# First block: TensorE's third exchanged first, a weight unit split sooner, one tap on ScalarE; last round of the last block by halves of the tokens

## The chip, the core and the metric

The kernel runs on one core of one Trainium2 chip. The metric is the device time of one execution in microseconds (us). Five engines work side by side, each through its own queue in program order: TensorE (PE in the profile; its weight loads stand as PEld), VectorE (DVE), ScalarE (ACT), GpSimd (POOL) and SyncE (SP), which here only issues transfers. Semaphores hold an instruction back until what it needs is done.

## The reference

A depthwise causal convolution over 4096 tokens with 7 taps, whose weights are a softmax for each of 8 heads, feeds a feed-forward layer with a gated activation. All is float32.

```python
B, S, D = 8, 4096, 192            # x; H, K = 8, 7; d_ff = 2048
w = softmax(weight)               # [8, 7], one row for 24 channels
out[b, s, c] = sum_k w[c // 24, k] * x_pad[b, s + k, c]
h = out.reshape(32768, 192) @ w_in          # [32768, 2048]
g = h * np.clip(h + 3, 0, 6) / 6
return g @ w_out                            # [32768, 192]
```

The weights of both products come as float64 and are brought to float32 on the chip from their two 32-bit words.

## The kernel before

The 32768 tokens go in 32 blocks of 1024, two halves of 512 tokens. x lies with channels on partitions: 64 partitions for the lower half of the tokens, 64 for the upper, and three "thirds" of 64 channels side by side in the free dimension (`y[:, 0..2]`). `swap(third)` (L273) exchanges the two partition halves through two DMAs on SyncE's queue (L276, L277), so that each half of the partitions holds the other half's tokens as well: OWN is what a partition half computed, OTHER is what it got.

**h of a block.** A product of h takes 64 rows of a weight unit against 512 tokens (`half_mm`, L302, matmul on L311); two such products, one on each half of the rows, run side by side. The result goes through ScalarE's relu (L317) and VectorE's gate (L321) into `g`. PSUM has eight banks, handed out by `take` and given back by `give` after the gate.

**The first block** is written out by hand, from L653 on. Its order is the program order of each engine:

- *Convolution.* The last third (`pe_third`) is convolved by TensorE: seven diagonal matrices, made by ScalarE (L670), times shifted x (L671); ScalarE copies the sum out of PSUM (L684). The other two thirds are convolved by VectorE, seven taps each in two halves of 256 tokens, so 14 steps a third (`per`): the first tap is a multiplication (L259), the others multiply and add (L263).
- *Weights.* 16 units, 8 of w_in and 8 of w_out. `split` is two VectorE operations (L174, L178), `clamp` three of ScalarE (L186, L189, L192), `join` two of VectorE (L195, L199), of which the second needs clamp's last result, and a product on GpSimd (L203), whose result the matmuls read. `load(n)` issues a unit's transfers on SyncE's queue.
- *Mixing.* The loop over `conv0` puts splits, clamps and joins between the taps: split(0) and clamp(0) before step 5, join(0) before step 11; before step 14 the copy of TensorE's third, the exchange of the first third and then of TensorE's, load(4), split(1) and clamp(1); before step 20 split(2), join(1), clamp(2); after the taps the exchange of the middle third, split(3), split(4), join(2), clamp(3).
- *First products.* Four parts (weight units 0 and 1, for OWN and for OTHER) take all eight banks; thirds come in `order = (0, pe_third, 1)`, the middle third last. After it come relu and gate for part after part, with a split, a join and a clamp beside some of them (`slots`, `between`), and twelve more parts, each with three pairs of products.

`out_direct` then makes the first block's output; the other blocks compute h by hand-written plans (`h_phase`) and the output by a seven-product scheme with fewer matmuls (`out_strassen`).

**The last block's output** is `out_last`. A round is one bank: four column tiles of 32 rows, each the sum of 8 matmuls (`mm`, L437) over 512 tokens, started in turn so that four run side by side (`side_by_side`). VectorE adds and subtracts rounds into c tiles (`add`, L541), `store` transposes 32x32 blocks (L547) and issues one DMA for each 32 channels (`store_rows`, L455). The last round is

```python
b, bank = three(3, 4, 2)
add(u2[:], u2[:], bank[m])                       # m: rows 0 to 95
store(i, u2, 0, 1, queues=both)                  # SyncE and ScalarE queues in turn
add(u3[rows(2)], u3[rows(2)], bank[rows(NQ)], ALU.subtract)   # rows 96 to 127
store(i, u3, 1, 0, range(2, 3), queues=both[::-1])
give(b)
```

Before it VectorE adds the quarters of product 5 (`pieces`), and stores `p5`.

Of the kernel before, what the change touches and what calls it, by code (L numbers as in the profile page):

```python
# [16 lines left out]
def kernel(  # L17
# [21 lines left out]
    nc = tc.nc  # L39
# [115 lines left out]
    class Rounding:  # L155
# [10 lines left out]
        def load(self):  # L166
            self.st = self.load_words()
# [105 lines left out]
    def swap(part):  # L273

        to = slice(OTHER + part.start, OTHER + part.stop)
        nc.sync.dma_start(out=y[D2:P, to], in_=y[0:D2, part])  # L276
        nc.sync.dma_start(out=y[0:D2, to], in_=y[D2:P, part])  # L277
# [19 lines left out]
    def take():  # L297
        return free_banks.pop(0)
# [131 lines left out]
    def dff_half(k):  # L430
        return g[:, :, k // G, k % G]

    def mm(bank, j, x, w, q, ps_, first, last):

        cols = slice(q * QS, (q + 1) * QS)
        return [
            lambda p=p: nc.tensor.matmul(  # L437
                out=bank[j * QS : (j + 1) * QS], lhsT=w_out[:, p, w, cols], rhs=x[:, p],
                start=(first and p == ps_[0]), stop=(last and p == ps_[-1]),
                tile_position=(0, j * QS),  # L440
            )
            for p in ps_
        ]

    def side_by_side(*streams):
        for mms in zip(*streams):
            for m in mms:
                m()

    every = range(NP)  # L450

    def store_rows(i, k, q, xt, j, dma=nc.sync):

        t0 = i * TB + k * N
        dma.dma_start(  # L455
            out=out[t0 : t0 + N, q * QS : (q + 1) * QS].rearrange("(t r) d -> r t d", r=QS),
            in_=xt[j * QS : (j + 1) * QS].rearrange("r (t d) -> r t d", d=QS),
        )

    def out_direct(i, work):  # L460
# [41 lines left out]
        5: (None, T1), 6: (S2, T2), 7: (S3, T3),  # L502
    }

    def product(bank, j, n, q, ks=every):
        x, w = prod[n]
        return mm(bank, j, S1 if n == 5 else x, w, q, ks, True, True)

    def four(*parts):

# [5 lines left out]
    def three(n, n4, q4):  # L516
        return four(*[(n, q) for q in range(NQ)], (n4, q4))
# [11 lines left out]
    def rows(q):  # L529
        return slice(q * QS, (q + 1) * QS)  # L530
# [9 lines left out]
    def add(out, x, y, op=ALU.add):  # L540
        nc.vector.tensor_tensor(out=out, in0=x, in1=y, op=op)  # L541

    def store(i, c, k, half_, qs=range(NQ), queues=(nc.sync,)):

        xt = ot.tile([P, N], F32, name="xt")
        r = slice(qs[0] * QS, (qs[-1] + 1) * QS)
        nc.vector.transpose(out=xt[r], in_=c[r])  # L547
        for q in qs:
            store_rows(i, k, half_ * NQ + q, xt, q, queues[q % len(queues)])

    def sums_tiles():
        return (cs.tile([DH, N], F32, name=f"c{k}") for k in range(6))
# [3 lines left out]
    def out_last(i):  # L556

        both = nc.sync, nc.scalar
        p1, p2, p4, p5, u2, u3 = sums_tiles()
        b, bank = three(1, 2, 0)  # L560
        nc.scalar.copy(out=p1[:], in_=bank[m])
        piece(p2, 0, bank, NQ)
        give(b)
        g_sums(nc.vector, (2,), every, 4)
        b, bank = four((2, 1), (2, 2), (4, 0), (4, 1))
        for dst, q, j in ((p2, 1, 0), (p2, 2, 1), (p4, 0, 2), (p4, 1, 3)):
            piece(dst, q, bank, j)
        give(b)
        g_sums(nc.vector, (4,), every, 4)
        add(p2[:], p1[:], p2[:])  # L570
        store(i, p2, 0, 0)
        b7, bank7 = three(7, 5, 0)
        piece(p5, 0, bank7, NQ)
        b, bank = three(6, 5, 1)
        piece(p5, 1, bank, NQ)
        add(u2[:], p1[:], bank[m])
        give(b)
        add(u3[:], u2[:], bank7[m])
        give(b7)
        two = slice(0, 2 * QS)  # L580
        add(p4[two], u3[two], p4[two], ALU.subtract)
        store(i, p4, 1, 0, range(2))
        b, bank = by_quarters(5, 2)
        pieces(p5, 2, bank)
        give(b)
        add(u2[:], u2[:], p5[:])
        add(p5[:], u3[:], p5[:])
        store(i, p5, 1, 1)
        b, bank = three(3, 4, 2)
        add(u2[:], u2[:], bank[m])  # L590
        store(i, u2, 0, 1, queues=both)
        add(u3[rows(2)], u3[rows(2)], bank[rows(NQ)], ALU.subtract)
        store(i, u3, 1, 0, range(2, 3), queues=both[::-1])
        give(b)

    def out_strassen(i, conv):
# [56 lines left out]
    with tc.manual_schedule():  # L653
        nc.vector.tensor_reduce(out=sm[:], in_=e_sb[:], axis=AX.X, op=ALU.add)
        nc.vector.tensor_scalar_add(sm[:], sm[:], 1e-9)
        nc.vector.reciprocal(sm[:], sm[:])
        nc.vector.tensor_tensor(
            out=c_sb[:], in0=e_sb[:], in1=sm[:].to_broadcast([P, KC]), op=ALU.mult
        )

        thirds = [slice(s, s + 1) for s in range(K3)]
        pe_third = K3 - 1
        b = take()
        for _ in range(3):

            nc.tensor.matmul(
                out=psum[:, b], lhsT=zeros[:, 0:P], rhs=zeros[:], start=True, stop=True
            )
        for k in range(KC):
            nc.scalar.mul(diag[:, k], ident[:], c_sb[:, k : k + 1])  # L670
            nc.tensor.matmul(  # L671
                out=psum[:, b], lhsT=diag[:, k], rhs=x_tiles[0][:, pe_third, k : k + N],
                start=(k == 0), stop=(k == KC - 1),
            )
        conv0 = conv_units(0, thirds[:pe_third], 2)
        per = len(conv0) // pe_third
        for k, u in enumerate(conv0):
            if k == 5:
                split(0)
                clamp(0)  # L680
            elif k == per - 3:
                join(0, more=False)
            elif k == per:
                nc.scalar.copy(out=y[:, pe_third], in_=psum[:, b])  # L684
                give(b)
                swap(thirds[0])
                swap(thirds[pe_third])
                load(AHEAD)
                split(1)
                clamp(1)  # L690
            elif k == per + 6:
                split(2)
                join(1)
                clamp(2)
            u()
        swap(thirds[1])
        split(3)
        split(4)
        join(2)
        clamp(3)  # L700


        parts = [(c, group) for p in range(0, NP, 2) for group in (OWN, OTHER)
                 for c in (p, p + 1)]
        early = [(c, group, (take(), take())) for c, group in parts[:4]]
        order = (0, pe_third, 1)
        for c in range(2):
            for slot, group, bs in early:
                if slot == c:
                    for s in order[:2]:  # L710
                        h_mm(c, group, bs, s, order)
        for c, group, bs in early:
            h_mm(c, group, bs, order[2], order)

        slots = [0, 1, 2, 3, 5, 6, 8, 10, 12, 14]
        n = 3
        for slot, (c, group) in enumerate(parts):
            first = slot < len(early)
            if first:
                bs = early[slot][2]  # L720
            else:
                bs = take(), take()
                for s in range(K3):
                    h_mm(c, group, bs, s)
            more = slot in slots

            def between():
                if more:
                    join(n)
                    clamp(n + 1)  # L730

            if slot == 6:
                x_tiles[1] = load_x(1)
            h_out(c, group, bs, (lambda: None) if first else between)
            if more:
                split(n + 2)
                if first:
                    between()
                n += 1
        while n < len(units):  # L740
            join(n)
            clamp(n + 1)
            split(n + 2)
            n += 1
        w_sums()
        start_pools.close()
        ss = ctx.enter_context(tc.tile_pool(name="ss", bufs=1))
        p5s = ctx.enter_context(tc.tile_pool(name="p5s", bufs=3))
        cs = ctx.enter_context(tc.tile_pool(name="cs", bufs=1))
        ot = ctx.enter_context(tc.tile_pool(name="ot", bufs=4))  # L750

        def conv_and_swap(i):
            return conv_units(i, [slice(0, K3)]) + [lambda: swap(slice(0, K3)), y_sums]

        out_direct(0, conv_and_swap(1))
        x_tiles[2] = load_x(2)

        S1 = ss.tile([P, NP, N], F32, name="s1")[:]
        left = []
        for i in range(1, NB):  # L760
            h_phase(left)
            if i + 1 < NB:
                left = out_strassen(i, conv_units(i + 1, [slice(0, K3)]))
            else:
                out_last(i)
            if i + 2 < NB:
                x_tiles[i + 2] = load_x(i + 2)
# [33 lines left out]
```

## Time and profile before

| | us |
|---|---|
| median of 6 runs (lowest to highest) | 2410.85 (2410.79 to 2410.95) |
| the profiled execution's own time | 2410.83 |
| its span, first to last instruction | 2409.0 |
| TensorE busy (share of the span) | 2398.3 (100%) |
| VectorE busy | 2088.1 (87%) |
| ScalarE busy | 1076.9 (45%) |
| GpSimd busy | 673.0 (28%) |
| TensorE's first product of h starts | 14.35 |
| first block's first output matmul starts | 58.75 |
| last matmul of the last round ends | 2402.79 |

A timeline line reads: start, length, engine, line, operation, output<-inputs, shapes, count, and in brackets the idle time of the engine before it with what ended it. The chain of waits is followed back from the last instruction: at each step to what released it, else to the instruction before it on its engine. The granted clock is the share of TensorE's full clock that it was given. A float32 matmul stands as two MATMUL records.

### The profile page before, as it was taken

To read this page: it belongs to the slowest core of one execution; us is meant where nothing else is said; L and a number is where in the kernel's file an instruction comes from. 1 tells how busy PE (TensorE), PEld (TensorE's weight loads), DVE (VectorE), ACT (ScalarE), POOL (GpSimd) and SP (SyncE) were. 2 spreads that over 40 slices of the span, in tenths; PEclk is the share of its full clock that TensorE was granted. 3 is DMA by queue.
4 is the path that set the end of the run, shared out by engine and by line. 5 is a ranking of instruction groups with operands and counts; after the bars stand their busy time and mean duration, and the time that the engine had idled before them with its cause. 6 is when DMAs were issued, how large, how long until landed. Compare 5 with 4: busy or idle time off the path is not lost.

```text
span 2409.0 us, 40076 instructions
## 1 busy us (share of the span) xinstructions
PE 2398.3 (100%) x16468; PEld 1009.2 (42%) x16468; DVE 2088.1 (87%) x2534; ACT 1076.9 (45%) x1827; POOL 673.0 (28%) x280
## 2 busy tenths in 40 slices
PE   9999999999999999999999999999999999999998
PEld 4334444334444344443444434444334444344433
DVE  8788888988888888898888898888898888888896
ACT  7234553345543355433454334553335543355433
POOL 2523321233221333122332223322233312333122
PEclk9999999999999999999999999999999999999999
DMA  5211122101122011221112211122201122111210
GB/s 145 40 25 29 27 40 40 39 18 26 39 41 40 19 35 27 40 41 22 32 27 40 41 34 22 27 40 40 40 18 34 30 40 40 21 34 27 40 27 14
DMA packets 227336, 84.65 MB, mean 35 GB/s; under 512 B 205456, under 2 KB 210576, under 8 KB 227152
## 3 DMA queue, kind: packets, MB, share of 16 engines
q1 hardware_dynamic: 225848, 81.56, 17.1%
q8 instruction: 129, 2.11, 0.4%
q14 instruction: 55, 0.45, 0.1%
q10 hardware_dynamic: 1208, 0.27, 0.1%
q0 software_dynamic: 96, 0.26, 0.0%
HBM read 31.72 MB, written 25.17 MB: 24 GB/s over the span
## 4 chain that ended last, share of the span: by engine, by line
PE 99%; DVE 1%; DMA 0%; issue 0%; ACTq 0%; SPq 0%; DVEq 0%
PE psum L311 50%; PE psum L437 48%; DVE y L263 0%; DMA x<-in_x_dram 0%; DMA y<-y 0%; DVE c L541 0%; ACTq L92 0%; DVE scale L174 0%; DVE y L259 0%; DVE scale L195 0%; DVE sig L199 0%; DVE top L178 0%; DVE xt L547 0%; SPq L276 0%; DVEq L259 0%
## 5 line engine op out<-in xcount | busy, mean ns | idle before, releaser
L437 PE MATMUL psum<-g,w_out 128*32 128x512 f32 x9312 | 1163.6, 592 | 0.0
L311 PE MATMUL psum<-y,w_in 64*128 64x512 f32 x3664 | 884.1, 591 | 3.0 <-DVE y L263 1.8
L497 POOL TENSOR_TENSOR s<-g 128x1024 f32<-128x1024 f32 x124 | 293.6, 2368 | 1644.7 <-DVE g L321 1644.7
L317 ACT ACTIVATE r<-psum,half 128x512 f32<-128x512 f32 x1024 | 641.2, 688 | 241.3 <-PE psum L311 234.1
L437 PEld LDWEIGHTS psum<-g,w_out 128*32 128x32 f32 x9312 | 337.4, 110 | 811.7 <-issue 770.2
L321 DVE SCALAR_TENSOR_TENSOR g<-r,psum 128x512 f32<-128x512 f32 x1024 | 641.2, 680 | 5.0 <-ACT r L317 1.1
L437 PE MATMUL psum<-s,w_out 128*32 128x512 f32 x1488 | 638.5, 592 | 0.0
L311 PEld LDWEIGHTS psum<-y,w_in 64*128 64x128 f32 x3664 | 430.2, 187 | 378.6 <-issue 298.8
L311 PE MATMUL psum<-y,w_in_t 64*128 64x512 f32 x1984 | 523.9, 592 | 0.0
L403 DVE TENSOR_TENSOR psum<-psum,p 128x512 f32<-128x512 f32 x496 | 324.5, 694 | 196.5 <-PE psum L311 187.5
L263 DVE SCALAR_TENSOR_TENSOR y<-x,c_sb,y 128x1536 f32<-128x1536 f32 (+1 forms) x210 | 416.7, 1992 | 6.6
L533 ACT COPY c<-psum 32x512 f32<-32x512 f32 x188 | 108.7, 578 | 600.7 <-PE psum L437 600.0
L497 POOL TENSOR_TENSOR g<-g 128x1024 f32<-128x1024 f32 x124 | 338.3, 2728 | 9.7
L311 PEld LDWEIGHTS psum<-y,w_in_t 64*128 64x128 f32 x1984 | 247.4, 186 | 194.0 <-issue 124.8
L541 DVE TENSOR_TENSOR c<-c,psum 32x512 f32<-32x512 f32 (+1 forms) x187 | 128.1, 685 | 81.6 <-ACT c L533 75.7
L396 ACT COPY psum<-psum 128x512 f32<-128x512 f32 x248 | 138.9, 571 | 72.5 <-PE psum L311 57.5
L437 PEld LDWEIGHTS psum<-s,w_out 128*32 128x32 f32 x1488 | 162.4, 110 | 1.2 <-issue 1.2
L399 ACT COPY p<-psum 128x512 f32<-128x512 f32 x248 | 133.2, 591 | 40.9 <-PE psum L311 40.1
L497 DVE TENSOR_TENSOR g<-s,g 128x2048 f32<-128x2048 f32 x62 | 139.3, 2286 | 3.9 <-POOL g L497 2.3
L497 DVE TENSOR_TENSOR g<-g 128x2048 f32<-128x2048 f32 x62 | 139.3, 2287 | 2.0 <-PE psum L437 1.0
L601 ACT COPY c<-psum 96x512 f32<-96x512 f32 x30 | 17.4, 581 | 174.5 <-PE psum L437 174.5
L606 ACT COPY c<-psum 96x512 f32<-96x512 f32 x30 | 17.4, 581 | 170.0 <-PE psum L437 170.0
(46 smaller groups left out, 433.2 us busy)
## 6 DMA issues: line engine op xcount, KB each, us to landing
out_dram<-xt SPq DMA_DIRECT2D x382, 64.0 KB, 2.0
y<-y SPq DMA_DIRECT2D x62, 384.0 KB, 4.9
x<-in_x_dram SPq DMA_DIRECT2D x55, 388.5 KB, 5.9
stage<-in_moe_w_in_dram SPq DMA_DIRECT2D x16, 192.0 KB, 4.4
stage<-in_moe_w_out_dram SPq DMA_DIRECT2D x8, 384.0 KB, 5.3
x<-in_x_dram SPq DMA_DIRECT2D x7, 384.0 KB
y<-y SPq DMA_DIRECT2D x6, 128.0 KB, 2.3
x<-in_x_dram SPq DMA_DIRECT2D x2, 128.0 KB, 4.4
```

What stands on the lines that cost most here:

```text
L263: nc.vector.scalar_tensor_tensor(out=to, in0=x[:, part, k + t : k + t + W], scalar=c, in1=to, op0=ALU.mult, op1=ALU.add,)
L311: nc.tensor.matmul(out=psum[:, b], lhsT=w[r], rhs=y[r, third_of_y], start=start, stop=stop, skip_group_check=onto,)
L317: nc.scalar.activation(r6, h, ACT.Relu, bias=half[:], scale=1.0 / 6.0)
L321: nc.vector.scalar_tensor_tensor(out=out, in0=r6, scalar=1.0, in1=h, op0=ALU.min, op1=ALU.mult)
L396: nc.scalar.copy(out=psum[:, bank["b"]], in_=psum[:, bank["a"]])
L399: nc.scalar.copy(out=self.p5[:], in_=psum[:, bank["e"]])
L403: nc.vector.tensor_tensor(out=psum[:, to], in0=psum[:, bank["b"]], in1=self.p5[:], op=ALU.add)
L437: lambda p=p: nc.tensor.matmul(out=bank[j * QS : (j + 1) * QS], lhsT=w_out[:, p, w, cols], rhs=x[:, p], start=(first and p == ps_[0]), sto ...
L497: engine.tensor_tensor(out=o[:, r], in0=a[:, r], in1=b[:, r], op=op)
L533: nc.scalar.copy(out=dst[rows(q)], in_=src[rows(j)])
L541: nc.vector.tensor_tensor(out=out, in0=x, in1=y, op=op)
L601: nc.scalar.copy(out=p1[:], in_=bank[m])
```

## The change

In the first block: ScalarE computes the first tap of the middle third for all 512 tokens (one instruction ahead of clamp(0)), and the two VectorE steps that did so are left out. Split(1), the copy of TensorE's third, its exchange and clamp(1) move ahead of the last three taps of the first third; the exchange of the first third and load(4) stay behind them. Join(1), split(2), clamp(2) come two taps into the middle third, join ahead of split. After the taps join(2) goes ahead of split(3), and clamp(3) ahead of split(4). The first products take TensorE's third first, then the first, then the middle one.

In the last block: the last round's matmuls are issued for tokens 0 to 255, then for 256 to 511, into the two halves of one bank, and adds, transposes and stores follow each half.

```diff
-    def mm(bank, j, x, w, q, ps_, first, last):
+    def mm(bank, j, x, w, q, ps_, first, last, tokens=slice(0, N)):
...
-                out=bank[j * QS : (j + 1) * QS], lhsT=w_out[:, p, w, cols], rhs=x[:, p],
+                out=bank[j * QS : (j + 1) * QS, tokens], lhsT=w_out[:, p, w, cols],
+                rhs=x[:, p, tokens],
...
-    def store(i, c, k, half_, qs=range(NQ), queues=(nc.sync,)):
+    def store(i, c, k, half_, qs=range(NQ), queues=(nc.sync,), tokens=slice(0, N)):
...
-        nc.vector.transpose(out=xt[r], in_=c[r])
+        nc.vector.transpose(out=xt[r, tokens], in_=c[r, tokens])
...
-        b, bank = three(3, 4, 2)
-        add(u2[:], u2[:], bank[m])
-        store(i, u2, 0, 1, queues=both)
-        add(u3[rows(2)], u3[rows(2)], bank[rows(NQ)], ALU.subtract)
-        store(i, u3, 1, 0, range(2, 3), queues=both[::-1])
+        b = take()
+        bank = psum[:, b]
+        for t in range(0, N, N // 2):
+            ts = slice(t, t + N // 2)
+            side_by_side(*[
+                product(bank, j, n, q, tokens=ts)
+                for j, (n, q) in enumerate([(3, 0), (3, 1), (3, 2), (4, 2)])
+            ])
+            add(u2[:, ts], u2[:, ts], bank[m, ts])
+            store(i, u2, 0, 1, queues=both, tokens=ts)
+            add(u3[rows(2), ts], u3[rows(2), ts], bank[rows(NQ), ts], ALU.subtract)
+            store(i, u3, 1, 0, range(2, 3), queues=both[::-1], tokens=ts)
         give(b)
...
+        nc.scalar.mul(y[:, 1], x_tiles[0][:, 1, 0:N], c_sb[:, 0:1])
         conv0 = conv_units(0, thirds[:pe_third], 2)
...
             elif k == per - 3:
                 join(0, more=False)
-            elif k == per:
+                split(1)
                 nc.scalar.copy(out=y[:, pe_third], in_=psum[:, b])
                 give(b)
-                swap(thirds[0])
                 swap(thirds[pe_third])
-                load(AHEAD)
-                split(1)
                 clamp(1)
-            elif k == per + 6:
+            elif k in (per, per + 1):
+                if k == per:
+                    swap(thirds[0])
+                    load(AHEAD)
+                continue
+            elif k == per + 4:
+                join(1)
                 split(2)
-                join(1)
                 clamp(2)
             u()
         swap(thirds[1])
+        join(2)
         split(3)
+        clamp(3)
         split(4)
-        join(2)
-        clamp(3)
...
-        order = (0, pe_third, 1)
+        order = (pe_third, 0, 1)
```

`store_rows` and `product` pass `tokens` on in the same way; its default is all 512 tokens.

More of the change, by code (lines that the diff above doesn't have):

```diff
@@ L450, with store_rows @@
     every = range(NP)
-    def store_rows(i, k, q, xt, j, dma=nc.sync):
+    def store_rows(i, k, q, xt, j, dma=nc.sync, tokens=slice(0, N)):
         t0 = i * TB + k * N
         dma.dma_start(
-            out=out[t0 : t0 + N, q * QS : (q + 1) * QS].rearrange("(t r) d -> r t d", r=QS),
-            in_=xt[j * QS : (j + 1) * QS].rearrange("r (t d) -> r t d", d=QS),
+            out=out[t0 + tokens.start : t0 + tokens.stop, q * QS : (q + 1) * QS].rearrange("(t r) d -> r t d", r=QS),
+            in_=xt[j * QS : (j + 1) * QS, tokens].rearrange("r (t d) -> r t d", d=QS),
         )
@@ L503, with product @@
     }
-    def product(bank, j, n, q, ks=every):
+    def product(bank, j, n, q, ks=every, **tokens):
         x, w = prod[n]
-        return mm(bank, j, S1 if n == 5 else x, w, q, ks, True, True)
+        return mm(bank, j, S1 if n == 5 else x, w, q, ks, True, True, **tokens)
     def four(*parts):
@@ L541, in add @@
         nc.vector.tensor_tensor(out=out, in0=x, in1=y, op=op)
-    def store(i, c, k, half_, qs=range(NQ), queues=(nc.sync,)):
+    def store(i, c, k, half_, qs=range(NQ), queues=(nc.sync,), tokens=slice(0, N)):
         xt = ot.tile([P, N], F32, name="xt")
         r = slice(qs[0] * QS, (qs[-1] + 1) * QS)
-        nc.vector.transpose(out=xt[r], in_=c[r])
+        nc.vector.transpose(out=xt[r, tokens], in_=c[r, tokens])
         for q in qs:
-            store_rows(i, k, half_ * NQ + q, xt, q, queues[q % len(queues)])
+            store_rows(i, k, half_ * NQ + q, xt, q, queues[q % len(queues)], tokens)
     def sums_tiles():
```

## The prediction

> **What bounds the kernel now.** I read the page's chain first, then the chain piece by piece, then the engine timelines of its two ends. The page's chain is TensorE almost alone.
>
> ```profile
> PE 99%; DVE 1%; DMA 0%; issue 0%; ACTq 0%; SPq 0%; DVEq 0%
> ```
>
> Piece by piece (start, length, what), TensorE runs from 25.21 us to 2402.83 without a stop; only the ends, which are what the change touches, hang on others.
>
> ```profile
> 21.77 0.47 DVE y L263
> 22.24 0.28 DVE scale L174
> ...
> 22.82 2.35 DMA y<-y
> 25.17 0.04 issue
> 25.21 33.60 PE psum L311 x152
> ...
> 2402.85 0.69 DVE c L541
> ```
>
> But 33.60 us hold 14 pairs of row halves up to 37.95 and 24 after it. A pair takes 0.857 (four MATMUL records, 0.428 per two), so the 14 need 12.0; they took 12.74. ScalarE's timeline from 22.55 shows why.
>
> ```profile
> 22.55 0.62 ACT L186 ACTIVATE sig<-scale,bias_e 128x384 f32<-128x384 uint32 x1 [3.54 <-DVE scale L174]
> ...
> 24.31 1.25 ACT L317 ACTIVATE r<-psum,half 128x512 f32<-128x512 f32 x2
> 25.45 0.61 ACT L186 ACTIVATE sig<-scale,bias_e 128x384 f32<-128x384 uint32 x1
> ...
> 28.35 0.60 ACT L186 ACTIVATE sig<-scale,bias_e 128x384 f32<-128x384 uint32 x1
> ...
> 35.90 2.40 ACT L317 ACTIVATE r<-psum,half 128x512 f32<-128x512 f32 x4
> ```
>
> From 22.55 until 40 ScalarE has no idle time: one clamp (1.76) and two relus (1.14) make 2.90 us a part, TensorE's part is 3 x 0.857 = 2.57, and all eight banks are taken. TensorE's ninth part started at 37.95, when the gate that follows the relus of 35.90 ended (37.89). So the end of the first block's h hangs on when ScalarE's clamp(3) starts, and that on VectorE's split(3).
>
> At the other end, VectorE:
>
> ```profile
> 2401.38 0.71 DVE L547 STREAM_TRANSPOSE xt<-c 96x512 f32<-96x512 f32 x1
> 2402.85 0.68 DVE L541 TENSOR_TENSOR c<-c,psum 96x512 f32<-96x512 f32 x1 [0.77 <-PE psum L437]
> 2403.57 0.71 DVE L547 STREAM_TRANSPOSE xt<-c 96x512 f32<-96x512 f32 x1
> 2404.31 0.69 DVE L541 TENSOR_TENSOR c<-c,psum 32x512 f32<-32x512 f32 x1
> 2405.04 0.70 DVE L547 STREAM_TRANSPOSE xt<-c 32x512 f32<-32x512 f32 x1
> ```
>
> It is free for the last round only from 2402.09, 0.77 before TensorE is done. Then four operations, ScalarE's store (issued 2405.77, landed 2407.55) and 1.45 of closing.
>
> **Sum.** The profiled execution took 2410.83 us (span 2409.0 and 1.83 around it); the median of six is 2410.85, so what I add to the one holds for the other.
>
> **The head.** VectorE's steps go by start to start. Removed: two L259 at 0.27, so -0.53. Added: ScalarE's multiplication, which waits for the middle third of x. Its second load is issued at 4.25 and lands within 5.0 (the longest of that line), at 9.25; clamp(0), the copy of TensorE's third and clamp(1) queue behind it. ScalarE takes 0.39 for 128 columns (L670) and 0.68 for 512 out of PSUM (L317); I take 0.65, 0.1 of it overlapped. Clamp(0) then starts at 9.9, not 8.73, and ends at 11.73, when join(0)'s second half (11.73) wants it: +0.05, between 0 and 0.3. The copy still starts at 12.58, when TensorE is done. Split(1) moved ahead of three taps costs VectorE nothing in sum.
>
> Two taps are stretched.
>
> ```profile
> L263 DVE SCALAR_TENSOR_TENSOR y<-x,c_sb,y x24: 471/474/1227, 7.2 to 21.8; 128x256 f32<-128x256 f32 x24
> ```
>
> The two of 1.2 us begin just after POOL's products of units 0 and 1 (12.36 and 18.41). Both products still meet taps, so 0.75 each is paid again: +0.05, between -0.75 and 0.3.
>
> Sum: the last tap ends some 0.4 earlier. But join(2) (0.94) now stands before split(3), which comes at 22.17 - 0.4 + 0.94 = 22.7, and clamp(3) at 23.1 instead of 22.55: **+0.55**. TensorE gains early: its third is ready at 13.2, unit 0's weights at about 13.9, so it starts near 13.9 (14.35 before), meets unit 1's weights at 18.8 (19.64) and the last exchange at 24.8 (25.21). All of that ends in the wait for banks, which now lasts 0.95 longer. SyncE's queue has the same transfers in the same order but for the two exchanges; they leave 0.9 sooner (TensorE's third, 13.2) and 0.7 later (the first third, 14.9), and load(4) behind them is not wanted before 23. Everything after the ninth part shifts whole: out_direct's first VectorE wait is for TensorE, 4.59 long, and takes the shift in.
>
> **The tail.** The first half of the last round takes 16 groups of four matmuls. Each now streams 256 columns: half of 0.428, 0.215, if the weights (0.13 for four) stay hidden; 0.343 if not, by the same rows. It runs from 2395.74 to 2399.2, and then lies waiting, for VectorE is busy until 2402.08. In the built program the first matmul of the second half waits on VectorE's count, for the value that the first half's 32-row add gives: halves of one bank don't overlap. So, with a 256-column add at 0.42 (2048 columns take 2.284, 512 take 0.687: 1.04 ns a column and 0.154) and a transpose at 0.44: 2402.11 + 0.42 + 0.44 + 0.42 + two gaps of 0.035 = 2403.46. Behind the waiting matmul stand the 31 others, and for them VectorE's last four operations. TensorE: 0.1 to start, 0.08 to fill, 16 x 0.215 = 3.44, 0.165 and 0.07 to leave (2402.18 + 0.43 to 2402.85): 2407.3. Four operations and gaps, 1.83: 2409.15. Issue and landing, 1.78 for 64 KB, between 0.89 and 1.78 for 32 KB, I take 1.6: 2410.8. Against 2407.55 that is **+3.2**. Seven operations at 0.35 (half) or 0.69 (nothing saved) make it +2.6 or +5.1.
>
> The Trainium skill ("PSUM — Partial Sum Buffer", Terms) calls TensorE writing a bank's quadrant while VectorE reads it a collision error. [...] No row of before has such a pair.
>
> **The clock.** TensorE now idles from 2399.2 to 2403.55, 4.3 us. The stretches (length, busy time of five engines' rows, granted clock, DMA) at the end of before:
>
> ```profile
> 2402.00:2405.00 3.00, 0.79 (x8) 0.00 (x0) 2.16 (x4) 0.00 (x0) 0.00 (x0) 1.00 0.42 66
> 2405.00:2406.00 1.00, 0.00 (x0) 0.00 (x0) 0.71 (x2) 0.00 (x0) 0.00 (x0) 0.76 0.71 107
> 2406.00:2407.00 1.00, 0.00 (x0) 0.00 (x0) 0.00 (x0) 0.00 (x0) 0.00 (x0) 0.50 0.93 135
> ```
>
> About 2.75 us after the last matmul (2402.78) the clock is halved. In the head, idle for 1.8 (12.55 to 14.35) didn't halve it. And from cold the matmuls on zeros go at 0.85 each from 1.50 on, and at 0.43 only after some 4.4 us. So 4.3 idle is enough for the drop in most runs. The price: nothing if it doesn't drop; if half pace lasts 4.4 from the restart, 2.2; I take 1.5, between a switch that comes at once and one that falls later or returns sooner: **+1.5**. By the Trainium skill ("TensorE: Matmul & The Clock Gate", What's actually happening) the gate looks at free-running windows of 3.4 us; an estimate from that figure is at most 1.7 where one whole window is slow, and varies with where the windows fall. The row alone gives 0 to 2.2.
>
> 2410.83 + 0.55 + 3.2 + 1.5 = 2416.1.
>
> **Rivals.**
> 1. The clock stays full: the idle stretch is cut by the gate's moment so that no drop comes. 2414.6, and within 0.2% of before: not slower. It decides at about 1.1 us of lost pace: the line of 0.2%, what a measurement of this kernel can tell from no change, is 4.82 us, at 2415.67. For it: idle may fall short of what the gate counts; against: 4.3 is well over 2.75.
> 2. TensorE, not ScalarE, sets the end of the head. Then the 0.4 is won, not 0.55 lost: 2415.1. For it: the chain of waits names the exchange at 25.17. Against: the 0.74 lost behind it.
> 3. Weights don't hide behind 256 columns: 16 x 0.128 = 2.05 more in the second half; TensorE then idles only 2.2, so the clock would hold: 2416.6, or 2418.1 if not.
> 4. The wait comes to nothing and the halves do overlap: VectorE then starts its eight operations at 2402.11 and ends at 2405.84 (before 2405.74), the store is 0.18 shorter; -0.1 in all, 2411.3. Against it stands the wait in the program.
>
> **Chances.** Forecast 0.52, rival 1 0.24, rival 2 0.12, rival 3 0.09, rival 4 0.03. The range leaves out rival 4 and the far ends of the operations' durations: 2414.0 to 2418.0. Slower by over 0.2%: most of the forecast (0.44), rival 3, a little of 2: 0.56. Within: 0.43. Faster: 0.01.
>
> **What would show it.** Head: split(3) after join(2) at about 22.7, ScalarE's idle-free stretch from 23.1, TensorE's long run from 24.8, out_direct at 59.3 (58.75). Tail: VectorE's 256-column add at 2402.7, a TensorE gap of 4 us ended by VectorE's L542, a clock below 1.00 after it, the last store issued near 2411. Wrong if the second half starts before VectorE has read the first, if the clock is 1.00 there, or if ScalarE has idle time between its first relu and 40 us.

## The result and the profile after

The changed kernel takes 2416.93 us (median of 16 runs, 2416.54 to 2417.93; one more on record took 2418.03), the kernel before beside it 2410.85 (2410.66 to 2411.15, 36 runs): 1.0026 of it, 95% interval [1.002, 1.0033], or 6.08 us slower. The profiled execution of after took 2416.54 (span 2414.8). Some lines have other numbers than before: the adds are L542, the transposes L548, the stores' DMAs L456, ScalarE's copy is L694, its tap L684.

The head first: VectorE's timeline of after, where the taps end.

```profile
21.96 0.54 DVE L195 SCALAR_TENSOR_TENSOR scale<-stage,scale 128x384 uint32<-128x384 uint32 x1
22.43 0.54 DVE L199 SCALAR_TENSOR_TENSOR sig<-top,sig 128x384 f32<-128x384 uint32 x1
22.90 0.35 DVE L174 TENSOR_SCALAR scale<-stage 128x384 uint32<-128x384 uint32 x1
```

The first step after the taps starts at 21.96 (22.17 before), but it is join(2), and split(3) follows it at 22.90. ScalarE's timeline of after shows what hangs on that.

```profile
23.28 0.62 ACT L186 ACTIVATE sig<-scale,bias_e 128x384 f32<-128x384 uint32 x1 [4.31 <-DVE scale L174]
...
25.03 1.25 ACT L317 ACTIVATE r<-psum,half 128x512 f32<-128x512 f32 x2
26.17 0.61 ACT L186 ACTIVATE sig<-scale,bias_e 128x384 f32<-128x384 uint32 x1
```

Clamp(3) starts at 23.28 instead of 22.55, 0.73 later, after an idle time that VectorE's split ended; from there ScalarE has no idle time until out_direct begins, and everything in the stretch is some 0.73 later. The chain of waits of after, in its parts at the two ends:

```profile
22.61 2.47 DMA y<-y
25.09 0.04 issue
25.13 34.42 PE psum L311 x152
...
2404.31 0.44 DVE c L542
2404.75 0.04 issue
2404.79 4.99 PE psum L437 x64
2409.79 0.02 issue
2409.81 0.43 DVE c L542
```

The last exchange lands 0.08 earlier than before (25.09 for 25.17), yet TensorE's run that follows takes 34.42 for the same 152 records that took 33.60. The time won ahead of the exchange is lost behind it, in waits for banks. At the other end the chain has a step that before's did not have: TensorE's last 64 records start when VectorE's 32-row add (2404.31) is done. VectorE's timeline of after:

```profile
2402.65 0.71 DVE L548 STREAM_TRANSPOSE xt<-c 96x512 f32<-96x512 f32 x1
2403.39 0.42 DVE L542 TENSOR_TENSOR c<-c,psum 96x256 f32<-96x256 f32 x1
...
2404.31 0.43 DVE L542 TENSOR_TENSOR c<-c,psum 32x256 f32<-32x256 f32 x1
2404.77 0.44 DVE L548 STREAM_TRANSPOSE xt<-c 32x256 f32<-32x256 f32 x1
2409.81 0.42 DVE L542 TENSOR_TENSOR c<-c,psum 96x256 f32<-96x256 f32 x1 [4.60 <-PE psum L437]
```

VectorE waits 4.60 for the second half, which TensorE could not start earlier. The stretches of after (length, busy time of TensorE, its weight loads, VectorE, ScalarE, GpSimd, then granted clock, DMA share, GB/s):

```profile
2400.40:2403.00 2.60, 0.24 (x8) 0.00 (x0) 2.46 (x5) 0.00 (x0) 0.00 (x0) 1.00 0.17 26
2403.00:2404.80 1.80, 0.01 (x1) 0.01 (x2) 1.67 (x5) 0.00 (x0) 0.00 (x0) 0.78 0.24 38
2404.80:2407.40 2.60, 2.60 (x28) 1.22 (x32) 0.41 (x1) 0.00 (x0) 0.00 (x0) 0.50 0.68 100
2407.40:2410.00 2.60, 2.33 (x44) 1.08 (x36) 0.19 (x1) 0.00 (x0) 0.00 (x0) 0.99 0.00 0
```

A record that crosses the edge of a stretch is counted on both sides. TensorE has next to nothing to do from 2400.6 to 2404.8, and the clock falls to half: the first six groups of four records of the second half start 0.43 apart, the ten from 2407.36 on 0.215 apart. The trace's clock records have half clock for 3.41, from 2404.02.

From the last round's start to the end of the span it is 17.79 in after and 13.26 before: 4.53 more. The other 1.27 of the span's growth were there at 2397.01, when that round starts (2395.74 before): 0.73 from the head, and 0.54 from a thing that no step of the prediction has. In the chain the pieces in which the middle blocks compute h, their phases of h, last 38.08, but for one of 38.43 before (at 1956.84) and three in after.

```profile
843.57 38.43 PE psum L311 x175
...
1363.79 38.28 PE psum L311 x175
...
1512.52 38.41 PE psum L311 x175
```

### The profile page after: what moved, and what is told of

Same layout as the page of the kernel before. It is cut to its first block, busy times and chain, and to the rows that moved or that the text cites. A ratio compares the mean times of both kernels' runs of the same rounds, so it can differ in the third digit from the quotient of the medians.

```text
span 2414.8 us, 40217 instructions
## 1 busy us (share of the span) xinstructions
PE 2400.4 (99%) x16532; PEld 1023.1 (42%) x16532; DVE 2088.2 (86%) x2536; ACT 1077.2 (45%) x1828; POOL 673.7 (28%) x280
## 3 DMA queue, kind: packets, MB, share of 16 engines
HBM read 31.72 MB, written 25.17 MB: 24 GB/s over the span
## 4 chain that ended last, share of the span: by engine, by line
PE 98%; DVE 1%; DMA 0%; SPq 0%; issue 0%; ACT 0%; DVEq 0%; ACTq 0%
PE psum L311 50%; PE psum L437 48%; DVE c L542 0%; DMA x<-in_x_dram 0%; DMA stage<-in_moe_w_in_dram 0%; SPq L137 0%; DMA y<-y 0%; DVE y L263 0%; SPq L103 0%; DVE xt L548 0%; DVE top L178 0%; SPq L92 0%; ACT y L684 0%; ACT scale L189 0%; SPq L277 0%
## 5 line engine op out<-in xcount | busy, mean ns | idle before, releaser
L437 PE MATMUL psum<-g,w_out 128*32 128x512 f32 (+1 forms) x9376 | 1165.2, 590 | 4.2 <-DVE c L542 4.2
L311 PEld LDWEIGHTS psum<-y,w_in 64*128 64x128 f32 x3664 | 439.9, 187 | 370.5 <-issue 287.0
L403 DVE TENSOR_TENSOR psum<-psum,p 128x512 f32<-128x512 f32 x496 | 324.5, 694 | 196.2 <-PE psum L311 184.9
L542 DVE TENSOR_TENSOR c<-c,psum 32x512 f32<-32x512 f32 (+2 forms) x189 | 128.4, 679 | 86.2 <-ACT c L534 76.3
```

The costliest lines, as they stand in the source:

```text
L311: nc.tensor.matmul(out=psum[:, b], lhsT=w[r], rhs=y[r, third_of_y], start=start, stop=stop, skip_group_check=onto,)
L403: nc.vector.tensor_tensor(out=psum[:, to], in0=psum[:, bank["b"]], in1=self.p5[:], op=ALU.add)
L437: lambda p=p: nc.tensor.matmul(out=bank[j * QS : (j + 1) * QS, tokens], lhsT=w_out[:, p, w, cols], rhs=x[:, p, tokens], start=(first and p ...
```

## Experiments

The theory from the prediction has three parts: ScalarE's chain, started by split(3), sets the head; halves of one bank come one after the other; TensorE's idle time then halves the clock. The rivals: the exchange sets the head; the clock has no part in it; the halves could overlap all the same. The longer phases came up on the way.

**Each end by itself.** e1_head_only has the edits to the first block and before's `out_last`; e2_tail_only the reverse.

> The head of the change alone, with the last round as before. Theory (ScalarE's chain of clamps and relus sets the end of the first block's h, and clamp(3) starts later because join(2) stands ahead of split(3)): 0.6 to 0.8 us slower than before, 2411.5 to 2411.7; ScalarE's stretch without idle time from about 23.2 (before 22.55), TensorE's first output matmul at about 59.4 (before 58.75). Rival (TensorE's wait for the last exchange sets it): the exchange lands some 0.1 to 0.4 sooner, so 2410.4 to 2410.8 and 58.3 to 58.7.

> The last round by halves alone, with the head as before. Theory (the second half's matmuls wait until VectorE has read the first half out of the same bank, and TensorE's clock falls meanwhile): 4.5 to 5.5 us slower than before, 2415.4 to 2416.3, and runs that lie over 1 us apart because the clock's fall comes at different moments. Rival (the two parts cost only together, since the head shifts the tail against the clock): under 4.

Measured beside before at 2410.82: the head alone 2412.03 (2411.93 to 2412.10, ratio 1.0005 [0.9996, 1.0014]), +1.21; the tail alone 2415.68 (2415.28 to 2416.98, ratio 1.0021 [1.0012, 1.003]), +4.86. Together 6.07, and the whole change costs 6.08: the ends add up. In the head alone out_direct starts at 59.49 (58.75 before) and the same three phases are long, at 843.57, 1363.77 and 1512.51; the tail alone has one, as before has.

**The wait for the bank.** e3_two_banks puts the second half of the last round into another bank, before's head kept. The diff is against the tail alone.

```diff
-        b = take()
-        bank = psum[:, b]
         for t in range(0, N, N // 2):
+            b = take()
+            bank = psum[:, b]
...
-        give(b)
+            give(b)
```

> The last round by halves as in the change, but each half in a bank of its own; head as before. Nothing makes the second half wait any more. Theory (the shared bank is the whole cost): within 0.2 us of before, 2410.65 to 2411.05, the first 256-column add at 2402.1 as soon as the transpose of p5 is done, VectorE's last transpose ending at 2405.8 (before 2405.74). Rival (matmuls of 256 columns cost by themselves, their weight loads standing bare): second half 2 us late, 2412.5 to 2414.

Measured: 2410.46 (2410.37 to 2410.55), ratio 0.9998 [0.999, 1.0007], 0.2 below the range expected. The halves as such cost nothing: 0.36 less than before, 5.2 less than with one bank. VectorE's timeline of this kernel:

```profile
2402.05 0.42 DVE L542 TENSOR_TENSOR c<-c,psum 96x256 f32<-96x256 f32 x1
...
2403.90 0.42 DVE L542 TENSOR_TENSOR c<-c,psum 96x256 f32<-96x256 f32 x1
...
2405.69 0.43 DVE L548 STREAM_TRANSPOSE xt<-c 32x256 f32<-32x256 f32 x1 [0.45 <-DMA out_dram<-xt]
```

The second half's add follows at once, with no idle time for TensorE. The last transpose now waits 0.45 for its xt buffer (the tile that `store` transposes into), which a store still reads. So the adds are not what made it faster than before: its last store is issued 0.39 later (2406.16 for 2405.77), but lands in 1.54 instead of 1.78, and the closing after that takes 0.9 instead of 1.45. Why the closing is shorter no run shows.

**The clock.** e4_warm is e2_tail_only with four matmuls of 128x512 more between the halves, into a spare bank that nobody reads, so that TensorE isn't idle as long.

> The last round by halves in one bank, head as before, and between the halves four extra matmuls of 128x128 weights and 512 columns into another bank whose result nobody reads: 3.4 us of work inside TensorE's idle 4.2. Theory (wait 3.2, fallen clock 1.3 to 1.5 on top): the clock stays full until the second half is done, 2413.9 to 2414.3, runs within 0.5 of each other. Rival (the clock costs nothing, the wait is all): as slow as the last round by halves without the extra matmuls, or slower.

Measured: 2414.23 (2413.84 to 2414.74), ratio 1.0014 [1.0005, 1.0023], +3.41. The chain of this kernel has the same step as after's:

```profile
2403.52 3.71 PE psum L437 x64
```

In the tail alone it is longer:

```profile
2403.48 5.39 PE psum L437 x64
```

The same 64 records take 3.71 at full clock, 4.99 in after and 5.39 in the tail alone, where half clock holds for eight groups of four instead of six: it lasts 3.41 in both, but in after 0.77 of it passes before the second half starts. By the medians the clock's part of the tail is 4.86 - 3.41 = 1.45, the wait's part 3.41; by these profiled runs the clock's part is 1.28 and 1.68. The times of e4 lie 0.9 apart, not within the 0.5 expected. Most of that lies outside the kernel's span: ten of its eleven spans are 2412.1 to 2412.2 and one is 2413.0, while those of the tail alone go from 2413.5 to 2415.2.

**The order after the taps.** e5_split_first is the head alone with one line moved; e6_join_first is before with the change's order of join, split and clamp and nothing else of it. The first diff is that of e5 against the head alone, the second that of e6 against before.

```diff
         swap(thirds[1])
-        join(2)
         split(3)
         clamp(3)
         split(4)
+        join(2)
```

```diff
         swap(thirds[1])
+        join(2)
         split(3)
+        clamp(3)
         split(4)
-        join(2)
-        clamp(3)
```

> The head of the change on the tail of before, but after the taps the order is split(3), clamp(3), split(4), join(2) instead of join(2), split(3), clamp(3), split(4). Theory (ScalarE's stretch without idle time, which begins with clamp(3), sets the end of the first block's h): split(3) comes at about 21.96 and clamp(3) at 22.34, join(2)'s 0.94 earlier than with the head alone; out_direct's first matmul at about 58.55 instead of 59.49, and the time about 2411.1 (2410.6 if the three longer phases of h that went with that head also go). Rival (the last exchange, landed at about 25.1 in both, sets it): out_direct stays at 59.4 to 59.5, the time at 2412.0.

> Before, with one edit: after the taps join(2) goes ahead of split(3), and clamp(3) ahead of split(4). Nothing else of the head is changed, so the exchange lands where it did (25.17). Theory (clamp(3) sets it): clamp(3) at 23.49 instead of 22.55, out_direct's first matmul at 58.75 + 0.94 = 59.69, the time at 2411.8. Rival (the exchange sets it): 58.75 and 2410.8. If the theory holds, the step cost more here than the whole head of the change did (0.74), and the rest of the head was worth what lies between.

Measured: e5 2411.09 (2411.00 to 2411.16, ratio 1.0001 [0.9992, 1.001]), 0.94 less than the head alone; e6 2411.78 (2411.71 to 2411.88, ratio 1.0004 [0.9995, 1.0013]; before beside them 2410.86). ScalarE's first step of the stretch in e5, then in e6:

```profile
22.33 0.61 ACT L186 ACTIVATE sig<-scale,bias_e 128x384 f32<-128x384 uint32 x1 [3.37 <-DVE scale L174]
```

```profile
23.49 0.62 ACT L186 ACTIVATE sig<-scale,bias_e 128x384 f32<-128x384 uint32 x1 [4.47 <-DVE scale L174]
```

out_direct starts at 58.51 in e5 and at 59.67 in e6. Clamp(3) moved by 0.94 in both and took out_direct with it, by 0.98 and 0.92, while TensorE's run from the exchange starts where it did (24.95 in e5, 25.00 in the head alone; 25.17 in e6, 25.21 in before). ScalarE's chain sets the end of the head; the exchange doesn't.

**The tap on ScalarE.** e7_tap_back is the head alone with the two L259 back on VectorE.

> The head of the change on the tail of before, but the middle third's first tap is back on VectorE (two L259) and off ScalarE. If the tap on ScalarE saved what two L259 take (0.53) less the 0.26 by which join(0) came later for it: the last tap ends 0.27 later, clamp(3) at 23.55 instead of 23.28, out_direct at 59.76, the time 2412.3. If it saved the whole 0.53: 60.0 and 2412.6. If it saved nothing, since POOL's products then fall beside other steps: 59.5 and 2412.0. The longer phases of h: if their places hang on how many instructions VectorE has run, which is here what it is in before, there is one of 38.43, at about 1957, and not the three at 843, 1363 and 1512, and the time is 0.5 less than said (2411.8).

Measured: 2411.80 (2411.74 to 2411.91, ratio 1.0004 [0.9995, 1.0013]), out_direct at 59.79. The tap on ScalarE saves 0.30 of its 0.53; and the phases are as in before, one of 38.43 at 1957.87.

**Making it faster.** e8_more_xt is e3_two_banks with eight xt buffers instead of four.

> The halves of the last round in two banks, as in e3_two_banks, with eight xt buffers instead of four. Theory: the last transpose waits 0.45 for a store that still reads its xt buffer; with more buffers VectorE's eight operations run back to back to 2405.7, the last store is issued at 2405.7 and lands at 2407.25, and the time falls by 0.45 to 2410.0. Rival (the stores' landing or the closing sets the end, not VectorE's last operation): 2410.4 to 2410.5, as with four buffers.

Measured: 2410.24 (2410.14 to 2410.38, ratio 0.9998 [0.9989, 1.0007]), half of the gain expected. The wait is gone (the last transpose starts at 2405.44), but in the profiled run out_direct came 0.16 later (58.91). ScalarE's first relu began at 24.43, not at 24.31, for it had to wait for TensorE, whose clock had fallen in the head. The stretch from 15.72 to 19.13 in before, then in e8 (columns as above):

```profile
15.72:19.13 3.41, 2.44 (x12) 0.60 (x8) 3.41 (x9) 2.40 (x5) 0.72 (x1) 1.00 0.86 204
```

```profile
15.72:19.13 3.41, 3.09 (x10) 0.90 (x8) 3.41 (x9) 2.39 (x5) 0.72 (x1) 0.50 0.86 208
```

TensorE had been idle for 1.94 until 14.36; in before an idle time of 1.80 at the same place left the clock full. How many of e8's other runs had this fall is not known.

e9_both takes both ends mended and spreads the work beside the first parts; e10_slots has that and before's head.

```diff
-        slots = [0, 1, 2, 3, 5, 6, 8, 10, 12, 14]
+        slots = [0, 1, 2, 4, 5, 7, 8, 10, 12, 14]
```

> The change's head with split(3), clamp(3) ahead of join(2), its tail in two banks with eight xt buffers, and the splits, joins and clamps beside the first block's parts spread: slots 0, 1, 2, 4, 5, 7, 8, 10, 12, 14 instead of 0, 1, 2, 3, 5, 6, 8, 10, 12, 14, so that ScalarE has a part without a clamp before banks are short. Theory (what is lost after the exchange is ScalarE's 2.90 a part against TensorE's 2.57): TensorE's run from the exchange (25.0) takes 33.60 - 0.74 = 32.9, out_direct at 57.9 (58.51 with the same order and the old slots), and the time 2411.09 - 0.6 in the head - 0.62 in the tail = 2409.9. Rival (something else, such as VectorE's gates or a unit that comes late, sets the banks): out_direct stays at 58.5, 2410.5.

> Before's head with the same spread slots, and the tail in two banks with eight xt buffers: none of the change's edits to the first block. Theory: out_direct at 58.0 to 58.1 (58.75 before), the time 2410.24 - 0.7 = 2409.5, the lowest of the series, since VectorE's stream has one longer phase of h and not three. Rival (the change's exchange order is worth something once ScalarE is out of the way): e9_both is the lower of the two by what out_direct is earlier.

Measured beside before at 2410.82: e9 2409.22 (2409.15 to 2409.44, ratio 0.9993 [0.9984, 1.0002]), e10 2410.20 (2410.11 to 2410.35, ratio 0.9998 [0.9989, 1.0006]). TensorE's run from the exchange in e9:

```profile
25.25 33.13 PE psum L311 x152
```

33.13, not the 32.9 expected: of the 0.74 that ScalarE cost in before, spreading the clamps won 0.47. But the run starts at 25.25, after an exchange that landed 0.3 later than e5's (24.95), so out_direct is only 0.20 earlier than there (58.31 for 58.51). In e10, with before's head, it starts at 58.25, 0.50 earlier than before. Both times were missed by 0.7, one below and one above, and most of that has another cause: e9 has no longer phase of h at all, e10 has two (38.46 at 99.6, 38.43 at 471.3). The rival of e10 is wrong too, since e9 is lower by 1.0 with an out_direct that is 0.06 later. e9 is the fastest kernel here, 1.6 below before.

**The longer phases.** In after, in the phase at 843.57, an L403 of VectorE (it adds two parts of h into a bank, and TensorE hangs on it) comes 0.35 late, all its inputs there:

```profile
865.79 1.30 DVE L403 TENSOR_TENSOR psum<-psum,p 128x512 f32<-128x512 f32 x2 [2.30 <-ACT p L399]
```

In the phases around it this step waits 1.95, not 2.30. Counted from the start, with the rows that only wait for a semaphore, it is VectorE's row 1216 of the trace, 19 x 64. In before the one that lengthens a phase is row 2752 (43 x 64), in e8 1600, in e10 192 and 704. e11 and e12 are before with two and three more issues of a memset of less than 0.1 in VectorE's idle time. The diff is e11's; e12 has the line once more.

```diff
     nc.vector.memset(bias_e[:, 0:1], float((1023 - 127 + 255) * EXP1))
+    nc.vector.memset(bias_e[:, 1:2], float(8 * 255 * EXP1))
+    nc.vector.memset(bias_e[:, 1:2], float(8 * 255 * EXP1))
     nc.vector.memset(bias_e[:, 1:2], float(8 * 255 * EXP1))
```

> Before, with the second VectorE memset of bias_e (L153, a stretch in which VectorE waits for its first load) issued three times instead of once; the result is the same. Theory of the longer phases of h: counted from the start, VectorE's rows whose number is a multiple of 64 come 0.35 late if VectorE had been waiting, and a phase is longer by that where such a row is the first L403 that TensorE hangs on. In before that is row 2752 (the phase at 1956.84), in the changed kernel rows 1216 and 2112 among others. Two rows more: row 2752 is no such L403 any more, and no other is; no phase of h after the first two is longer than 38.10, and the time falls by 0.35 to 0.41, to 2410.45. Rival (the places have to do with time, an address or chance): the phase at 1957 stays longer, 2410.82.

> Before, with the same memset issued four times: one row more than in e11_two_memsets. Theory: three L403 that VectorE waited for now have numbers that are multiples of 64, those at about 344.8, 577.1 and 1003.8, in the phases of h that start at 323.0, 545.8 and 991.4. These three last 38.28 to 38.43 instead of 38.08, the one at 1957 doesn't, and the time is 0.8 to 1.05 over that of two memsets: 2411.3 to 2411.5. Rival: 2410.8, as before, since one memset of less than 0.1 in VectorE's idle time costs nothing.

Measured beside before at 2410.79 (2410.66 to 2410.95): two memsets 2410.48 (2410.37 to 2410.59, ratio 0.9999 [0.999, 1.0008]), with no longer phase; three 2410.80 (2410.72 to 2410.91, ratio 1.0 [0.9991, 1.0009]), with one, at 545.80, not three. The same step in e11, then in e12 (L405 and L406 are L403 moved down by the lines put in):

```profile
577.12 1.30 DVE L405 TENSOR_TENSOR psum<-psum,p 128x512 f32<-128x512 f32 x2 [1.96 <-PE psum L313]
```

```profile
577.46 1.30 DVE L406 TENSOR_TENSOR psum<-psum,p 128x512 f32<-128x512 f32 x2 [2.31 <-ACT p L402]
```

So the place in VectorE's stream decides, and one memset moves 0.35 us. But the rule put down was too wide: of the three rows it named in e12, 832 (13 x 64) was late, 512 and 1408 (8 and 22 x 64) were not. Over the kernels here each late row is an odd multiple of 64 (192, 704, 832, 1216, 1600, 2112, 2752, 3008), and the even multiples for which VectorE had waited over 1 us were on time (384, 512, 1024, 1408, 2816). Nor is every odd one late. Row 64 of after starts 0.02 after the relu that it waits for, although VectorE had stood for 1.68:

```profile
25.73 0.69 DVE L321 SCALAR_TENSOR_TENSOR g<-r,psum 128x512 f32<-128x512 f32 x1 [1.68 <-ACT r L317]
```

Row 576 of e12 (9 x 64) was on time after 2.15, and row 1600 of e11 after 0.26, while row 1600 of before was late by 0.35 where VectorE otherwise waits only 0.13. What sets them apart is the row ahead: ahead of each late row stands one that only waits for a semaphore, ahead of each of these odd ones on time a calculation or a transpose. This narrower rule was read from the runs afterwards and was not tried on a new one. After's third long phase (38.28) fits it from another engine: there ScalarE's relu at 1380.78 is late by 0.28, its row 1472, 23 x 64. What happens at these rows the profile doesn't show.

## Why the prediction was right

Forecast 2416.1, measured 2416.93, slower by 0.26% (the interval begins at 0.20%); the sum +5.25 against +6.08. Without the longer phases, which no step foresaw, it would be some 2416.4, still above the line of 2415.67. The parts:

| term | forecast | measured |
|---|---|---|
| head, out_direct later | +0.55 | +0.73 (after), +0.74 (head alone) |
| longer phases of h | none | +0.5 (chain of after) |
| wait for the bank | +3.2 | +3.4 (e4) |
| clock | +1.5 | +1.45 (tail alone less e4) |

**Head.** The step that decided it, join(2) ahead of split(3), was priced at 0.94, and cost 0.92 by itself in e6 and gave back 0.98 in e5. Rival 2, in which the exchange decides, is excluded by both. The size was off by 0.18 in one term, what the taps save: the step after them starts 0.21 earlier, not 0.4. From join(0)'s second half (11.99, before 11.73) to there after takes 9.97 against 10.44, which is the 0.48 forecast. The rest was lost ahead of that: the first tap starts 0.11 later (6.73 for 6.62; 6.62 in e6, which keeps before's start, 6.73 in e7, which has the tap on VectorE, so the tap isn't its cause), and the wait of join(0) for ScalarE, taken at 0.05 (0 to 0.3), was 0.15. ScalarE's tap took 0.72 and started at 9.48, against 0.65 and 9.25. Of the two stretched steps one turned out to be split(1)'s L178 (12.73, 1.16 long, beside GpSimd's product of 12.63) and one a tap; together they cost what was forecast.

**Tail.** The wait, its cause and its place were as forecast: the add ends, TensorE starts, VectorE stands for 4.60. At full clock the second half takes 3.71 in e4; the sum had 3.69. Rival 4 (the halves overlap) is excluded by the chain, rival 3 (weights that don't hide) by the groups of the first half, which follow each other every 0.215. e3 shows that the wait was the bank's and not the halves': with a bank each they cost less than nothing.

By the Trainium skill ("PSUM — Partial Sum Buffer", PSUM bank collisions raise a hardware error) two engines may use one bank at once in different quadrants. By that the second half's first three products needed to wait only for the 96-row add, 0.9 earlier than for the 32-row add that released them here. No run here tried it.

**Clock.** It fell, as the forecast had it, for 3.41 by the trace's records; rival 1 (it stays full) is excluded by after and by e2, and e4 shows its price with the idle time taken away. That the price came out so near is luck in part: 1.5 was picked between 0 and 2.2, and the two profiled runs show 1.28 and 1.68. The spans of after's runs go from 2414.8 to 2416.3. The prediction's row of the head, idle for 1.8 without a fall, was no safe bound either: in e8 1.94 was enough.

By the Trainium skill ("TensorE: Matmul & The Clock Gate", What's actually happening) the gate looks at windows of 3413 ns that run free of the kernel; the record of 3.41 agrees. An estimate from that figure was at most 1.7; 4.99 against 3.71 in the traces makes it 1.28, 5.39 against 3.71 makes it 1.68, the medians 1.45.

**Not foreseen.** The 0.5 of the longer phases. They came with two instructions fewer on VectorE, in blocks that no edit touches, and stand in no term of the sum.

## What to carry to other kernels

Before a round is cut in halves so that its reader can start sooner, see whether the reader is free then, and give each half its own bank: in one bank the second half here waited for the reader of the first, and TensorE, idle for 4.15 meanwhile, paid 1.3 to 1.7 more at half clock. Where an engine runs without idle time behind one first step, that step's place in its supplier's queue is the time of the whole stretch: put the supplier's short work for it ahead of all else, and spread what can wait. Differences of 0.3 to 1 us in 2400 can come from where in an engine's stream a step falls, so read the middle of the chain too before a gain is put down to an edit.

## What the hardware showed that was not expected

In these runs a row of VectorE's trace whose number is an odd multiple of 64, and which follows a row that only waits for a semaphore, came 0.35 to 0.40 later than its inputs; odd multiples behind a calculation or a transpose were on time. Where VectorE is still busy meanwhile it doesn't show. Whether it costs time depends on whether TensorE hangs on that row: between none (e9, e11) and three (after) of some thirty phases, 0.2 to 0.37 each. ScalarE's rows showed the same, 0.28 each (704, 1344 and 1472 in after, 2496 in before); only 1472 lengthened a phase.

An idle time of TensorE of 1.94 halved its clock for 3.41 in e8, and one of 1.80 at the same place left it full in before.
